# Head 0's first loads on the hardware queues, head 1's on GpSimd's, the block list ahead of both, and two mask transfers later

## The chip, the cores and the metric

The kernel runs on one core of one Trainium2 chip. The core has a matrix engine (TensorE, "PE" in the profile), a vector engine (VectorE, "DVE"), a scalar engine with activation functions (ScalarE, "ACT"), GpSimd ("POOL") and SyncE ("SP"). SP, ACT and GpSimd can each issue transfers (DMAs) to 16 DMA engines that they share. SP's and ACT's transfers go through hardware queues and copy data as it is; GpSimd's go through a software queue and may convert the type on the way, here from fp32 in memory to bf16 on the chip. The metric is the device time of one execution in microseconds (us), lower is better; the median of three runs before the change is 204.28 us.

## The reference

Block-sparse attention (BigBird's pattern) followed by a gated feed-forward layer with a short convolution. Sizes: batch 4, 8 heads, 768 tokens, head dimension 64, blocks of 32 tokens (24 blocks), three sampled blocks for each block; model width 512, inner width 1024.

```python
scores = (1/sqrt(D)) * q @ k.T                    # per batch and head
mask = |blk_i - blk_j| <= 1  or  blk_i, blk_j in {0, 23}
mask |= kb in sampled_blocks[qb]                  # the block list
attn = softmax(where(mask, scores, -1e9)) ;  a = attn @ v
x = a as (B, S, 512)
h = relu(x @ w_in)
conv = sum_k conv_w[k] * shift(h, k - 1)          # along the tokens
out = (h * sigmoid(conv)) @ w_out
```

## The kernel before, in words

**Units.** The 32 heads are handled as 16 pairs (4 batches of 4 pairs). For a pair, the scores are computed transposed, a 128x128 tile of (keys, queries) at a time; eight such tiles fill a tile `st` of 128x1024 and are one *unit*. A unit is: matmuls into `st` (line L746 of the profile), one exponential on ACT from `st` to `pt` (L757), and eight matmuls of `pt` with the values into `av` (L779). There are 144 units; a pair takes four and a half of them for the first half of the queries and as many for the second, and a unit is called by its number below (unit 0 is the first). Two `st` tiles alternate, so the scores of unit u can be written once the exponential of unit u-2 is done.

**The mask.** The mask is not applied after the scores but multiplied in. The tiles `e` and `o` hold, for one pair, keys and queries transposed (64 rows of features) and below them 24 more rows, one for each block: on the key side these rows say which blocks may not be looked at, on the query side they hold -8000 at the token's own block. The key side is made from the block list `sbi` on DVE (`a_rand`, L284 and L286, then `k_rows`, L314), the query side from `nblk` (`q_rows`, L300). Tiles `e` and `o` exist five times (slots 0 to 4, `e_67` to `e_71` and `o_72` to `o_76`). Slot 0's mask rows are computed, slot 1's copied on DVE (L358), and slots 2 to 4 are filled by six transfers that SP issues (L361, `m_dma`), 72 KB each. Pair 4, the first in slot 4, is needed from unit 36 on.

**The first loads.** Pair 0's queries and keys come as fp32 through the hardware queues into tiles `o2s`: SP issues head 0's keys (`k0`), then the block list, then the convolution's weights; ACT issues both heads' first 384 queries (`q0`) and then head 1's keys (`k1`). Four casts on ACT (`cast`, L328 as every copy of `dcopy`) turn them into the bf16 tile `nat_88`. All the other loads, pair 1's keys first, are GpSimd's (all recorded at L241), one after the other in an order fixed by `in_turn`.

**Transposes.** Keys and queries of pairs 0 to 4 are transposed on PE (keys L470, queries L508) into PSUM (`mix` or `av`) and copied from there into `e` and `o` by ACT or DVE (L328 or L330). Later pairs are transposed by transfers of SP (L585).

**The rest.** When the values of a pair are summed, DVE normalizes them (L696, L698), the result is transposed (L707 by SP, L717 by PE) and goes through the first feed-forward matmul (L895), the relu (L915 on ACT or L917 on DVE), the convolution and gate (L949 to L1006) and the second matmul (L825), whose result goes out. These steps run among the units of later pairs.

**What sets the order.** Every step is an `op` in a graph, and the table `ORDER` lists the steps by number, with the engine and the buffer where there is a choice. `put_down` writes the program in that order, so each engine's instructions stand in a fixed row and wait for each other by semaphores. On PE the first row is 44 `warm` matmuls of a zero tile (L1027), and 12 `fill` matmuls (L1034) stand among the first units.

## Time and profile before

| what | before |
|---|---|
| median of 3 runs | 204.28 us (203.92 to 204.41) |
| the profiled execution's own time | 204.64 us |
| its span, first to last instruction | 202.9 us |
| PE busy | 196.4 us, 97% |
| ACT busy | 188.0 us, 93% |
| DVE busy | 179.9 us, 89% |
| mean busy share of the DMA engines, 5 to 45 us | over 0.9 in most slices |

The span leaves out 1.74 us of the execution (204.64 less 202.9), which lie before the first and after the last instruction. Starts in the profile count from the span's start. In a row of the timeline stand start, length, engine, line, operation, written tile<-read tile, shape and count; in brackets the engine's idle time just before, and what ended it. Rows that hold several instructions run from the first one's start to the last one's end. "Busy" of PE contains the modelled time that a matmul takes through the array, so short gaps of PE do not show in it.

### The profile page before, as it was taken

The numbers are of one execution on the slowest core, as the hardware profiler recorded it, in microseconds if no ns is written. First come the engines' busy times: TensorE is split into PE (matmuls) and PEld (weight loads), VectorE is DVE, ScalarE is ACT, GpSimd is POOL, SyncE is SP. The second block draws the span as 40 slices with busy tenths as digits, with TensorE's granted clock in tenths as the row PEclk, the third lists the DMA queues.
The fourth block names the chain that finished last, engine by engine and source line by source line (L and its number), as shares of the span: only waits on it lengthen the run. The fifth ranks groups of instructions, "written<-read, shape, count | busy, mean of one in ns | idle before, by whom it ended". The sixth has DMA issues, their size and how long they took to land.

```text
span 202.9 us, 6808 instructions
## 1 busy us (share of the span) xinstructions
PE 196.4 (97%) x2707; PEld 153.6 (76%) x2707; DVE 179.9 (89%) x574; ACT 188.0 (93%) x247; POOL 56.3 (28%) x108
## 2 busy tenths in 40 slices
PE   7898999999999999999999999999999999999993
PEld 7797888897788777877688877776678877776742
DVE  8965989999999978999899988999899968999950
ACT  5898999999999999999999998999999989998842
POOL 8940789300621363102534328400000000000000
PEclk9999999999999999999999999999999999999999
DMA  6999999995879399947969699995331202001515
GB/s 147 167 217 200 179 178 186 192 145 118 120 117 143 75 120 157 212 108 154 128 103 165 71 214 211 123 155 137 93 116 23 42 14 68 13 11 58 200 62 206
DMA packets 53711, 26.11 MB, mean 129 GB/s; under 512 B 39624, under 2 KB 50592, under 8 KB 53680
## 3 DMA queue, kind: packets, MB, share of 16 engines
q0 software_dynamic: 19984, 11.24, 43.3%
q1 hardware_dynamic: 33136, 13.92, 34.9%
q10 hardware_dynamic: 560, 0.52, 0.7%
q8 instruction: 21, 0.34, 0.7%
q14 instruction: 10, 0.08, 0.1%
HBM read 23.08 MB, written 6.29 MB: 145 GB/s over the span
## 4 chain that ended last, share of the span: by engine, by line
PE 74%; ACT 14%; DMA 5%; POOL 3%; issue 3%; DVE 0%; ACTq 0%
PE st L746 23%; PE mix L895 18%; PE mix L825 17%; PE av L779 13%; ACT pt L757 12%; DMA nat<-in_q_dram 5%; POOL nat L241 2%; POOL vn L241 1%; PE mix L810 1%; PE st L825 1%; ACT m L998 1%; PE av L970 1%; ACT hE L915 1%; PE mix L508 1%; ACT o2s L328 0%
## 5 line engine op out<-in xcount | busy, mean ns | idle before, releaser
L757 ACT ACTIVATE pt<-st 128x1024 bf16<-128x1024 f32 x144 | 140.4, 1037 | 2.4 <-PE st L746 1.2
L779 PE MATMUL av<-vt,pt 128*128 128x65 bf16 x1152 | 59.7, 193 | 0.0
L779 PEld LDWEIGHTS <-pt 128*128 128x128 bf16 x1152 | 52.1, 97 | 9.9 <-ACT pt L757 0.3
L895 PE MATMUL mix<-xT,winb 128*128 128x384 bf16 (+2 forms) x288 | 53.7, 308 | 0.1
L949 DVE TENSOR_SCALAR m<-hE,cw 128x382 bf16<-128x382 bf16 (+2 forms) x192 | 49.4, 317 | 0.5 <-ACT hE L915 0.2
L825 PE MATMUL mix<-woutb,gT 128*128 128x512 bf16 x176 | 47.1, 379 | 0.0
L746 PE MATMUL st<-o 88*128 88x128 bf16 (+1 forms) x240 | 44.2, 229 | 0.4 <-ACT pt L757 0.3
L746 PE MATMUL st<-o,e 88*128 88x128 bf16 (+1 forms) x228 | 43.3, 233 | 0.2 <-ACT pt L757 0.2
L746 PE MATMUL st<-e,o 88*128 88x128 bf16 (+1 forms) x224 | 42.5, 234 | 0.5 <-ACT pt L757 0.5
L746 PE MATMUL st<-e 88*128 88x128 bf16 (+1 forms) x208 | 40.9, 239 | 0.3 <-ACT o L328 0.3
L746 PEld LDWEIGHTS <-o 88*128 88x128 bf16 x464 | 34.7, 97 | 8.4 <-issue 1.6
L746 PEld LDWEIGHTS <-e 88*128 88x128 bf16 x436 | 32.6, 97 | 7.0 <-ACT e L328 0.4
L959 DVE TENSOR_TENSOR m<-m 128x764 bf16<-128x764 bf16 (+2 forms) x64 | 33.6, 532 | 0.4
L895 PEld LDWEIGHTS <-winb 128*128 128x128 bf16 x288 | 23.9, 97 | 7.8 <-issue 0.5
L998 ACT ACTIVATE m<-m 128x764 bf16<-128x764 bf16 (+2 forms) x32 | 26.3, 830 | 0.5 <-DVE m L959 0.3
L417 POOL COPY pace<-pt 1x1 bf16<-1x1 bf16 x24 | 6.4, 267 | 56.1 <-ACT pt L757 56.0
L825 PEld LDWEIGHTS <-gT 128*128 128x128 bf16 x184 | 15.2, 97 | 8.7
L1006 DVE TENSOR_TENSOR gT<-m,hE 128x764 bf16<-128x764 bf16 (+3 forms) x36 | 18.1, 511 | 0.5
L698 DVE TENSOR_TENSOR xtok<-av,rcp 128x384 bf16<-128x384 f32 (+2 forms) x36 | 18.2, 506 | 0.3
L917 DVE TENSOR_SCALAR hE<-mix 128x384 bf16<-128x384 f32 x29 | 15.9, 550 | 2.5 <-PE mix L895 2.1
L915 ACT ACTIVATE hE<-mix 128x384 bf16<-128x384 f32 (+2 forms) x35 | 17.2, 508 | 0.7 <-PE mix L895 0.5
L241 POOL DMA_DIRECT2D nat<-in_q_dram x23 | 16.9, 736 | 2.7 <-issue 2.3
(80 smaller groups left out, 155.7 us busy)
## 6 DMA issues: line engine op xcount, KB each, us to landing
out_dram<-o2s SPq DMA_DIRECT2D x23, 256.0 KB
vn<-in_v_dram POOLq DMA_DIRECT2D x16, 192.0 KB, 5.6
nat<-in_k_dram POOLq DMA_DIRECT2D x15, 192.0 KB, 5.4
nat<-in_q_dram POOLq DMA_DIRECT2D x7, 192.0 KB, 5.2
winb<-in_moe_w_in_dram POOLq DMA_DIRECT2D x2, 512.0 KB, 11.7
woutb<-in_moe_w_out_dram POOLq DMA_DIRECT2D x4, 256.0 KB, 6.2
nat<-in_q_dram POOLq DMA_DIRECT2D x8, 96.0 KB, 4.6
nq<-in_q_dram POOLq DMA_DIRECT2D x5, 96.0 KB, 5.4
```

The source lines that it names most:

```text
L241: return op(name, {eng: occ}, lambda e: on(e).dma_start(out=dst(), in_=src), prio, deps, dma=(kind, service), **kw)
L698: nm = op("norm", {"DVE": t_dps(128 * C)}, lambda e: nc.vector.tensor_tensor(out=xtok_t[xk.index][:, 0:C].rearrange("p c h d -> p h c d"), ...
L746: nc.tensor.matmul(out=st[:, 128 * x:128 * (x + n_)], lhsT=QK[kc % 2][s][0:88, 1, hh, kc // 2, :], rhs=QK[par][s][0:88, 0, hh, idx:idx + n ...
L757: nc.scalar.activation(out=pt_t[ptb.index], in_=st_t[stb.index], func=AF.Exp, bias=0.0, scale=0.125)
L779: nc.tensor.matmul(out=o[:, off:off + 65], lhsT=pt_t[ptb.index][:, 128 * x:128 * x + 128], rhs=V_t[vslot_b[P].index][:, hh, kc, 0:65], sta ...
L825: nc.tensor.matmul(out=acc(), lhsT=gT_t[gb.index][:, ffc, 128 * t:128 * t + 128], rhs=woutb[:, ffc, :], start=(ffc == 0), stop=(ffc == NFF ...
L895: nc.tensor.matmul(out=mix_t[hb.index][:, w1 * y:w1 * y + w1], lhsT=winb[:, fc, 128 * ffc:128 * ffc + 128], rhs=xT_t[xt_buf[n].index][:, f ...
L915: i = nc.scalar.activation(out=dst, in_=src, func=AF.Relu, bias=0.0, scale=0.5)
L949: i = nc.vector.tensor_scalar(out=m_t[cb.index][:, x, y, 0:w], in0=hE_t[heb.index][:, f0 + y, t0 + x:t0 + x + w], scalar1=cw[:, x, f0 + y: ...
L959: nc.vector.tensor_tensor(out=m[:, a_, :, 0:w], in0=m[:, a_, :, 0:w], in1=m[:, b_, :, 0:w], op=ALU.add)
L998: th = [op("tanh", {"ACT": t_act(2 * w) + 0.04}, lambda e, cb=cb, w=w: nc.scalar.activation(out=m_t[cb.index][:, 0, :, 0:w], in_=m_t[cb.in ...
L1006: i = nc.vector.tensor_tensor(out=gT_t[gtb.index][:, f0:f0 + 2, t0:t1], in0=m_t[cb.index][:, 0, :, 0:w], in1=hE_t[heb.index][:, f0:f0 + 2, ...
```

## The change

Five things change.

1. SP issues the block list first and, behind it, head 0's queries alone (128x192 fp32, 96 KB). ACT issues head 0's keys as its only load.
2. Head 1's first queries and keys become GpSimd's first two loads and arrive as bf16 in `nat_88`. Two of the four casts are gone.
3. Before slot 4's two mask transfers stands a new step `slot_mem`: GpSimd writes two elements into `e_71` and `o_76`, so these transfers wait until GpSimd has come that far.
4. The table `ORDER` is another one. It differs up to unit 39 or so, and is the same from there on (the last difference on PE is row 1443 of 5415). In it pair 0's query rows of `e` go from DVE to ACT, the copies for the last batch's mask (`mlast`) go from the start to behind pair 3's copies, and one relu goes from DVE to ACT (28 instead of 27 on ACT of 128x384, 28 instead of 29 on DVE).
5. The code is four lines shorter above the units, so line numbers in the changed program are lower by 4 to 10 (L746 becomes L742, L757 L753, L508 L504, L328 L320, L361 L355).

```diff
 ORDER = """
-00010w0y020A0407080506q/1r0r10zr2r3030VA30ar4r5r6r7r80xr9rarb0drc1d0rdrerfrgrh090b0fV0gV0j0nVrirjrk0mVrlrm1ern
+00010w0y020A04050607q/109r0r1r2r3r403r5r6r70ar8r9rarb0brcrd0cre0T3rf08rgrh0U0Brirjrk1d00drl0g0eArm0WArn0fV0VA
...
-    qf, kf = o2s_t[0], [o2s_t[1], o2s_t[2]]
-    def first_q(e, prio, after):
-        return dma("ld_q0", e, lambda: qf[:, 0:384].rearrange("p (h c) -> p h c", h=2),
-                   q[0, 0:2, 0:384].rearrange("h (p c) d -> p h (c d)", p=128), prio, service=0.7, earliest=1.0, after=after)
-
-    def first_k(x, e, prio, after):
-        return dma("ld_k0", e, lambda: kf[x][:, 0:384], k[0, x].rearrange("(p c) d -> p (c d)", p=128), prio,
-                   service=0.75, earliest=1.0, after=after)
-
-    k0 = first_k(0, "SP", -22, [])
-    q0 = first_q("ACT", -22, [])
-    k1 = first_k(1, "ACT", -21, [q0])
+    qf, kf = o2s_t[0], o2s_t[1]
+    k0 = dma("ld_k0", "ACT", lambda: kf[:, 0:384], k[0, 0].rearrange("(p c) d -> p (c d)", p=128), -22,
+             service=0.75, earliest=1.0)
     ld_sb = op("ld_sb", {"SP": 0.46}, lambda e: nc.sync.dma_start(out=sbi, in_=sampled_blocks.bitcast(I32)), -21,
-               after=[k0], lat=1.8)
-    ld_q0, ld_k0 = [q0, q0], [k0, k1]
-    ld_cw = dma("ld_cw", "SP", lambda: cw0, moe_conv_w.rearrange("k (f p) -> (k f) p", p=128), 8, service=0.05, after=[ld_sb])
+               lat=1.8)
+    q0 = dma("ld_q0", "SP", lambda: qf[:, 0:192], q[0, 0, 0:384].rearrange("(p c) d -> p (c d)", p=128), -22,
+             service=0.5, earliest=1.0, after=[ld_sb])
+    ld_cw = dma("ld_cw", "SP", lambda: cw0, moe_conv_w.rearrange("k (f p) -> (k f) p", p=128), 8, service=0.05, after=[q0])
...
     for s in range(1, NSLOT):
-        mr = []
+        mr, late = [], []
+        if s == 4:
+            late = [op("slot_mem", {"POOL": 0.2}, lambda e, s=s: [nc.gpsimd.tensor_copy(out=t[s][64:65, 0, 0, 0, 0:2], in_=warm[64:65, 0:2]) for t in (E_t, O_t)], T(14), [o_warm])]
...
-                             T(4.5 * s - 2.5) + 0.1 * x, [m_h1[x], m_kh[x]] + m_k[1:] * x, dma=("hw", 0.6)))
+                             T(4.5 * s - 2.5) + 0.1 * x, [m_h1[x], m_kh[x]] + m_k[1:] * x + late, dma=("hw", 0.6)))
...
         if P == 0:
-            both = {"ACT": 0.42, "DVE": 0.47}
-            cq = [cast("cast_q", lambda x=x: nat_t[nb.index][:, 0, 192 * x:192 * x + 192],
-                       lambda x=x: qf[:, 192 * x:192 * x + 192], -16.5 + 2 * x, [ld_q0[x]], {"ACT": 0.25, "DVE": 0.28},
-                       uses=[nb]) for x in range(2)]
-            ck = [cast("cast_k", lambda x=x: nat_t[nb.index][:, 1, 384 * x:384 * x + 384], lambda x=x: kf[x][:, 0:384],
-                       -16.6 + 2 * x, [ld_k0[x]], both, alloc=[] if x else [nb],
-                       uses=[nb] if x else [])
-                  for x in range(2)]
-            ld_k, ld_q = ck, cq
+            lq = dma("ld_q1", "POOL", lambda: nat_t[nb.index][:, 0, 192:384],
+                     q[0, 1, 0:384].rearrange("(p c) d -> p (c d)", p=128), -22, service=0.3, kind="sw", alloc=[nb])
+            lk = dma("ld_k1", "POOL", lambda: nat_t[nb.index][:, 1, 384:768],
+                     k[0, 1].rearrange("(p c) d -> p (c d)", p=128), -21, service=0.55, kind="sw", uses=[nb])
+            in_turn("first", lq)
+            in_turn("first", lk)
+            cq = cast("cast_q", lambda: nat_t[nb.index][:, 0, 0:192], lambda: qf[:, 0:192], -16.5, [q0],
+                      {"ACT": 0.25, "DVE": 0.28}, uses=[nb])
+            ck = cast("cast_k", lambda: nat_t[nb.index][:, 1, 0:384], lambda: kf[:, 0:384], -16.6, [k0],
+                      {"ACT": 0.42, "DVE": 0.47}, uses=[nb])
+            ld_k, ld_q = [ck, lk], [cq, lq]
```

The order moves instructions at three places that the prediction speaks of. The first is the start of GpSimd's row, from the identity matrix to the queries of pair 3 (`nat_88` is pair 0's natural layout, `nat_85`, `nat_86` and `nat_87` are pairs 1, 2 and 3, `vn` holds values). Before:

```order
L263 AFFINE_SELECT ident<-ident 128x128
L241 DMA nat_85<-in_k_dram 128x2x384
L261 IOTA colidx_i 24x24
L241 DMA nat_85<-in_q_dram 128x2x192
L241 DMA vn_92<-in_v_dram 128x2x384
...
L241 DMA nat_87<-in_q_dram 128x2x192
```

And now:

```order
L255 AFFINE_SELECT ident<-ident 128x128
L241 DMA nat_88<-in_q_dram 128x192
L253 IOTA colidx_i 24x24
L241 DMA nat_88<-in_k_dram 128x384
L241 DMA nat_85<-in_k_dram 128x2x384
L241 DMA nat_85<-in_q_dram 128x2x192
L241 DMA vn_92<-in_v_dram 128x2x384
...
L241 DMA nat_87<-in_q_dram 128x2x192
```

Two loads stand ahead of pair 1's keys, and every later load is issued two places further back; pair 3's queries were the ninth load and are the eleventh.

The second is the start of ACT's row, up to the exponentials of the first units (`pt_96` is unit 0's, `pt_97` unit 1's; `mix` and `av` hold transposed keys and queries of pair 0). Before:

```order
L241 DMA o2s_125<-in_q_dram 128x2x192
L241 DMA o2s_127<-in_k_dram 128x384
L328 ACT_TABLE_LOAD
L328 CAST nat_88<-o2s_126 128x384
L328 CAST nat_88<-o2s_125 128x192 x2
L328 CAST nat_88<-o2s_127 128x384
L328 COPY e_67<-mix_65 64x384
L328 COPY e_67<-mix_66 64x256
L328 COPY o_72<-mix_66 64x128
L328 COPY o_72<-mix_65 64x384
L328 COPY e_67<-av_63 64x256
L757 ACTIVATE pt_96<-st_61 128x1024
```

And now:

```order
L241 DMA o2s_126<-in_k_dram 128x384
L290 ACT_TABLE_LOAD
L290 ACTIVATE e_67<-nblk 24x256
L290 ACTIVATE e_67<-nblk 24x128
L320 CAST nat_88<-o2s_126 128x384
L320 CAST nat_88<-o2s_125 128x192
L320 COPY e_67<-mix_65 64x384
...
L320 COPY o_72<-mix_65 64x384
L753 ACTIVATE pt_96<-st_61 128x1024
L320 COPY e_67<-av_64 64x384
L753 ACTIVATE pt_97<-st_62 128x1024
```

One load and two casts are gone, two small mask activations have come, and the copy that stood ahead of unit 0's exponential is now behind it, with head 1's keys in place of its queries.

The third is PE's row around the transposes of pair 3's queries (`nat_87`). Weight loads, which stand ahead of every matmul, are left out, and so are further matmuls of the same kind. Before:

```order
L746 MATMUL st_61<-o_74,e_69 128x128
...
L746 MATMUL st_61<-e_69,o_74 128x128
L508 MATMUL mix_66<-ident,nat_87 128x128
...
L779 MATMUL av_63<-vt_78,pt_103 128x65
...
L779 MATMUL av_63<-vt_78,pt_96 128x65
L746 MATMUL st_62<-e_69,o_74 128x128
```

And now:

```order
L742 MATMUL st_62<-e_69,o_74 128x128
...
L742 MATMUL st_62<-o_74,e_69 128x128
L775 MATMUL av_64<-vt_79,pt_97 128x65
...
L504 MATMUL mix_66<-ident,nat_87 128x128
...
L742 MATMUL st_61<-e_69 128x256
```

The transposes stood between the scores of unit 10 (`st_61`) and those of unit 11 (`st_62`); they now stand between unit 11's and unit 12's (`st_61` again), and no matmuls into `av` stand between them and unit 12's scores any more, where eight stood before unit 11's.

80 lines of the change are left out of this document (40 added, 40 removed).

## The prediction

> **What bounds the kernel now.** I read the page first, then the chain of waits in order of time, then the timeline of the first 20 us, and last the transfers by their time to landing.
>
> ```profile
> span 202.9 us, 6808 instructions
> PE 196.4 (97%) x2707; PEld 153.6 (76%) x2707; DVE 179.9 (89%) x574; ACT 188.0 (93%) x247; POOL 56.3 (28%) x108
> ```
>
> The two engines that bound it together are PE and ACT. By stages (columns: busy time of PE, its weight loads, DVE, ACT and POOL, then the granted clock, the share of the DMA engines and GB/s), they have little left from 18 us on, and nothing from 26 us:
>
> ```profile
> 18.00:26.00 8.00, 7.69 (x150) 7.13 (x147) 6.41 (x23) 7.36 (x9) 4.20 (x7) 1.00 1.19 185
> 26.00:40.00 14.00, 14.00 (x199) 11.44 (x196) 13.29 (x43) 13.81 (x18) 10.20 (x23) 1.00 1.33 187
> 40.00:60.00 20.00, 20.00 (x299) 16.01 (x298) 19.44 (x55) 19.95 (x25) 3.33 (x8) 1.00 0.95 132
> ```
>
> So a microsecond won or lost before 20 us reaches the end, since the work after unit 39 is the same in the same order. The chain of waits begins with loads (start, length, what):
>
> ```profile
> 1.41 0.83 POOL nat L241
> ...
> 7.33 10.12 DMA nat<-in_q_dram
> 18.13 0.46 PE st L746 x6
> ```
>
> GpSimd issues its loads one after the other, and pair 3's queries, issued at 7.33, land at 17.45. The timeline shows what that costs, and what comes first (start, length, then the idle time before in brackets):
>
> ```profile
> 0.74 0.40 SPq L241 DMA_DIRECT2D o2s<-in_k_dram  x1
> 3.78 1.61 ACT L328 CAST nat<-o2s 128x384 bf16<-128x384 f32 x4 [0.73 <-DMA o2s<-in_k_dram]
> 4.34 0.48 PE L470 MATMUL mix<-ident,nat 128*128 128x128 bf16 x3
> 5.29 0.73 ACT L328 COPY e<-mix 64x384 bf16<-64x384 bf16 x2
> 6.05 0.64 ACT L328 COPY o<-mix 64x128 bf16<-64x128 bf16 x2
> 6.32 0.27 PE L746 MATMUL st<-e 88*128 88x256 bf16 x1 [0.26 <-ACT o L328]
> 7.36 0.37 ACT L328 COPY e<-av 64x256 bf16<-64x256 bf16 x1 [0.67 <-DVE o L330]
> 7.63 10.39 ACT L757 ACTIVATE pt<-st 128x1024 bf16<-128x1024 f32 x11
> 17.49 0.40 PE L508 MATMUL mix<-ident,nat 128*128 128x128 bf16 x4 [0.64 <-DMA nat<-in_q_dram]
> 18.67 1.02 ACT L757 ACTIVATE pt<-st 128x1024 bf16<-128x1024 f32 x1 [0.64 <-PE st L746]
> ```
>
> Two places decide. At the start ACT waits 0.73 us for head 0's keys, works through four casts and four copies, waits 0.67 us for DVE, and starts unit 0 at 7.63. Eleven exponentials then run without a gap, about 0.92 us apart. At 17.49 PE gets pair 3's queries late and ACT loses 0.64 us before unit 11 at 18.67; unit 12 follows 0.92 us later, at 19.59.
>
> **The start, part by part.** The sum is made on the profiled execution, 204.64 us, of which 202.9 are span; the median of the runs is 0.36 us lower, and I take the change off the median.
>
> Head 0's keys move from SP's queue to ACT's, where they are still the first thing issued. They landed just before 3.78, three microseconds after their issue, and I let them land at the same time; with half the bytes beside them it could be 0.3 us earlier, behind the other queue 0.4 us later. Two of four casts go: half of 1.61 is 0.80, so ACT would be free at 4.58, but PE's key transposes end at 4.34 + 0.48 = 4.82, and the copies start at 4.85 instead of 5.29. They take the same 1.40 us (5.29 to 6.69), so ACT is done at 6.25. Unit 0's scores start when the third copy is done, 5.88 instead of 6.32; from there to the last of unit 0's matmuls 0.6 us pass, so unit 0's exponential starts at about 6.5, 1.1 us earlier. The copy of 0.37 us that stood ahead of it with its wait on DVE now stands behind it, on 384 columns instead of 256, and holds up unit 1: 6.5 + 0.92 + 0.38 = 7.8, against 7.63 + 0.92 = 8.55. **From unit 1 on the start is worth 0.75 us** (0.35 to 1.05 by the landing of the keys).
>
> The mask rows that ACT takes over (`q_rows`, 24x256 and 24x128) run while ACT waits for the keys; ahead of them ACT loads a table:
>
> ```profile
> 1.76 1.28 ACT L328 ACT_TABLE_LOAD   x1 [1.76 <-issue]
> ```
>
> The table load ended at 3.04 and now comes some 0.5 us earlier because one issue ahead of it is gone, so 1.2 us are idle for two operations that took DVE 0.47. If that cover were gone, they would cost their length. DVE hides the rest, and only just:
>
> ```profile
> 2.23 0.47 DVE L300 TENSOR_SCALAR e<-nblk 24x256 bf16<-24x256 bf16 x2
> ...
> 3.17 0.66 DVE L344 TENSOR_SCALAR mlast<-nblk 24x128 bf16<-24x128 bf16 x3
> ...
> 4.74 0.21 DVE L284 TENSOR_TENSOR hit<-colidx_i,sbi 24x72 f32<-24x72 int32 x1
> ...
> 10.53 0.77 DVE L330 COPY o<-mix 64x256 bf16<-64x256 bf16 x2
> ```
>
> DVE works with hardly a gap up to 11.3, where pair 1's last copy ends; unit 4, whose second half needs the copy before it, started at 7.63 + 4 x 0.92 = 11.3. In the change unit 4 is wanted 0.75 us earlier, and DVE has 0.47 + 0.66 = 1.13 us less to do before, so it keeps up with 0.4 us to spare. This needs the block list before the compare (L284). It is issued at 0.74 now; even if it landed only when the keys did, just before 3.78, the compare would run 0.9 us earlier than at 4.74, which is still enough. Zero in the sum.
>
> **Head 1 on GpSimd.** Two loads, of 48 and 96 KB as bf16, go ahead of pair 1's keys. What GpSimd's loads cost (KB, and microseconds from issue to landing), first in an empty queue late in the kernel, then the loads issued at 1.41 (pair 1's keys), 6.62 (pair 3's keys) and 7.33:
>
> ```profile
> nq<-in_q_dram POOLq DMA_DIRECT2D x1, 96.0 KB, 2.9
> nat<-in_k_dram POOLq DMA_DIRECT2D x1, 192.0 KB, 3.8
> ...
> nat<-in_k_dram POOLq DMA_DIRECT2D x1, 192.0 KB, 4.7
> nat<-in_k_dram POOLq DMA_DIRECT2D x1, 192.0 KB, 7.3
> nat<-in_q_dram POOLq DMA_DIRECT2D x1, 96.0 KB, 10.1
> ```
>
> Head 1's keys, issued second at about 2.34, land between 5.2 (empty queue) and 7.0 (as pair 1's keys did). PE wants them behind unit 0's scores, at 6.5; unit 1 is due at 7.8 and needs 0.4 us of transposes and 0.45 of scores ahead, so they are hidden up to 6.9, and I add nothing.
>
> **Pair 3's queries.** They move from the ninth load to the eleventh. From pair 1's keys (landed 6.1) to pair 3's (13.9) 1152 KB came in, 148 KB for each microsecond; so 144 KB more are at most 0.97 us. It is less where GpSimd starts on a freer queue: pair 1's keys are then issued two issues (1.6 us) later, at 3.0, and land at 6.8 if they take the 3.8 of an empty queue, 0.7 us later, or 0.3 us later if the queue fills faster. Against that stand the two mask transfers of slot 4, 144 KB, which no longer come into this stretch; they cancel the whole 0.97 if they were moved ahead of or beside pair 3's queries, and give nothing if they queued behind. Ends: 0.65 us earlier (0.3 less 0.97) and 0.97 later. The stretch around their landing is the busiest one:
>
> ```profile
> 8.00:12.00 4.00, 3.46 (x60) 3.24 (x58) 3.71 (x10) 4.00 (x5) 3.53 (x6) 1.00 1.24 172
> 12.00:16.00 4.00, 4.00 (x83) 3.72 (x81) 2.12 (x8) 3.89 (x5) 0.92 (x2) 1.00 1.36 231
> ```
>
> GB/s go from 172 to 231 there though GpSimd issued only two more loads, so something else, and the masks are all that is open, moves beside pair 3's queries and not after them. I take the end near cancellation: 0.2 us later, 17.65.
>
> The Trainium skill has a rule on this ("DMA: Bandwidth & Descriptors", section "Queues, rings and completion order"): each DMA engine takes packets in turn from all the queues that have work for it. By it the masks take turns with pair 3's queries whenever they were issued, the landing would not move from 17.45, and the sum would come to 203.3; with strict order of issue it would be 18.4 and 204.3. The stretch of 231 GB/s agrees with turns.
>
> What hangs on it: unit 11 started 18.67 - 17.45 = 1.22 us after the landing, with the eight `av` matmuls (0.25 us) between. Now unit 12 comes in this place without them: 17.65 + 0.97 = 18.6. Without any wait unit 12 would start at 19.59 - 0.64 - 0.75 = 18.2. So 0.4 us of the wait stay, and **at unit 12 the kernel is 19.59 - 18.6 = 1.0 us ahead.**
>
> **One relu more on ACT.** Between unit 12 and unit 39 ACT does one relu that DVE did:
>
> ```profile
> 40.69 0.51 ACT L915 ACTIVATE hE<-mix 128x384 bf16<-128x384 f32 x1
> 41.06 1.96 ACT L757 ACTIVATE pt<-st 128x1024 bf16<-128x1024 f32 x2
> ```
>
> It takes 0.37 us of ACT (40.69 to 41.06). It costs nothing where PE holds ACT up, and all of it where ACT is the bound; in the stage from 26 to 40 us ACT has 0.19 us idle, and I take 0.2 of 0.37. The `slot_mem` step, two copies of two elements on GpSimd, and the wait of the later mask transfers cost nothing: behind them on SP stands only a transpose that ran at 38.11, and slot 4 is needed from unit 36 on. The first and the last mask transfer and that transpose were issued here:
>
> ```profile
> 7.10 0.89 SPq L361 DMA_DIRECT2D e<-e  x1
> ...
> 11.07 0.71 SPq L361 DMA_DIRECT2D o<-o  x1
> ...
> 38.11 1.30 SPq L707 DMA_TRANSPOSE xT<-xtok  x1
> ```
>
> **Sum:** 1.0 less 0.2 is 0.8 us: 203.8 in the profiled execution, **203.5 us** as the median.
>
> **Rivals.**
>
> *The wait eats it all* (20%). Pair 3's queries land at 18.4, with nothing won from the masks. Unit 12 starts at 19.4 and 0.2 us are left, which the relu takes: 204.3. For it: nothing but queue order is needed. Against it: the stretch of 231 GB/s.
>
> *The masks go ahead of pair 3's queries, slower* (13%). The masks of slots 2 and 3 wait for DVE (the first one was issued at 7.10, the others 0.8 us apart), which is now a microsecond earlier, while pair 3's queries are issued 1.4 us later. In order of issue only one mask stood ahead of them; now four do, 216 KB more, 1.46 us at 148 KB. The landing goes to 17.45 + 0.97 + 1.46 = 19.9, unit 12 to 20.85, 1.26 us behind, and with the relu the time is 205.7. It decides from a landing of 18.4 on, where unit 12 comes no earlier than before, and from 19.0 on the kernel is measurably slower.
>
> *No wait remains* (8%). The load lands by 17.2 and unit 12 starts at 18.2, 1.4 us ahead: 202.9, or 202.6 if the keys come 0.3 us earlier.
>
> *A colder matrix engine* (4%). The first row of `warm` matmuls is 25 long and no longer 30, so PE idles 0.6 us before its first transposes, at 4.34, and no longer 0.16:
>
> ```profile
> 1.06 3.12 PEld L1027 LDWEIGHTS <-warm 128*128 128x128 bf16 x30 [1.06 <-DVE warm L225]
> 6.71 0.49 PEld L1027 LDWEIGHTS <-warm 128*128 128x128 bf16 x7
> ```
>
> A `warm` takes 0.104 us at first and 0.07 or less from about 5 us on, though the row of the granted clock shows nothing of it. If the faster pace came later, units 0 and 1 would take twice their 0.46 us, about 0.9 us in all, and the time would be 204.4. The Trainium skill ("TensorE: Matmul & The Clock Gate", section "What's actually happening") says that the clock opens after a window of some 3.4 us in which PE was busy, and starts anywhere in it; whether an idle 0.6 us matters it does not say, and no row here shows it.
>
> **How the numbers follow.** My forecast has 55%, its own range is 202.8 to 203.9. A measurement here can tell about 0.3%, 0.61 us: faster is below 203.67, slower above 204.89. Faster: 52 of the forecast's 55 and the 8 without a wait, 0.60. Same: 3, 20 and 4, 0.27. Slower: 0.13. The range of 202.6 to 204.8 leaves out most of the slower rival and little below.
>
> **What would show it.** In the changed profile: casts that start near 3.8 and two fewer; unit 0 at about 6.5 and unit 1 at 7.8; the compare before 3.8; pair 3's transposes after a wait, at 17.7, and unit 12 at 18.6; from there to the end the same distance as before plus 0.2 us. I am wrong if unit 1 starts after 8.2 (keys late), if unit 4 waits for DVE (list late), or if pair 3's queries land after 18.4.

## The result, and the profile after

The change makes the kernel slower, by 0.67%. The median is 205.69 us (205.01 to 206.26, five executions) against 204.2 (203.92 to 204.41) for the kernel before beside it; the ratio is 1.0067, 95% interval 1.0042 to 1.0092. The forecast was 203.5 in a range of 202.6 to 204.8. Timed once more (e17), the change had a median of 205.32 us, ratio 1.006 (1.0029 to 1.0091). Some executions of either kernel took over 1.5% longer than the fastest of their kernel; medians, ranges and ratios leave them out.

The profiled execution is the slowest of the five, 206.26 us. The page has PE and ACT no busier than the longer span explains, and DVE less busy than before:

```profile
span 204.5 us, 6815 instructions
PE 197.8 (97%) x2707; PEld 154.5 (76%) x2707; DVE 178.5 (87%) x571; ACT 188.7 (92%) x248; POOL 56.9 (28%) x112
```

The timeline of the changed kernel up to 16 us (start, length, then the idle time before in brackets):

```profile
3.24 0.77 ACT L320 CAST nat<-o2s 128x384 bf16<-128x384 f32 x2 [0.15 <-DMA o2s<-in_k_dram]
4.10 0.95 PE L1023 MATMUL st<-warm 128*128 128x128 bf16 x7
5.44 0.37 ACT L320 COPY e<-mix 64x256 bf16<-64x256 bf16 x1 [0.63 <-PE mix L504]
5.70 0.89 SPq L355 DMA_DIRECT2D e<-e  x1
5.95 0.42 PE L742 MATMUL st<-e 88*128 88x256 bf16 x1
7.05 1.02 ACT L753 ACTIVATE pt<-st 128x1024 bf16<-128x1024 f32 x1 [0.58 <-PE st L742]
8.33 5.70 ACT L753 ACTIVATE pt<-st 128x1024 bf16<-128x1024 f32 x6
13.98 0.40 PE L504 MATMUL mix<-ident,nat 128*128 128x128 bf16 x4 [0.89 <-DMA nat<-in_q_dram]
15.03 2.01 ACT L753 ACTIVATE pt<-st 128x1024 bf16<-128x1024 f32 x2 [1.00 <-PE st L742]
```

The keys came early (ACT waited 0.15 us, not 0.73), but seven `warm` matmuls stand between the transposes of the keys and those of the queries, and PE was slow: unit 0's first score matmul took 0.42 us here and 0.27 before. Unit 1 started at 8.33, not at 7.8. Then six exponentials ran without a gap, and at unit 7 ACT lost 1.00 us, because **pair 2's** queries were not there. The chain of waits shows them as its longest piece by far:

```profile
5.59 0.85 POOL nat L241
6.44 7.49 DMA nat<-in_q_dram
13.93 0.05 issue
13.98 0.40 PE mix L504 x4
...
19.94 0.83 ACT pt L753
```

Issued at 6.44, they landed at 13.93. Before, they were issued at 5.19 and landed 5.7 us later, at 10.9 (transfers by size and time to landing):

```profile
nat<-in_q_dram POOLq DMA_DIRECT2D x1, 96.0 KB, 5.7
```

Pair 3's queries, on which the forecast hung, landed at 16.3, and nothing waited for them. The first mask transfer was issued at 5.70, ahead of pair 2's queries; before, at 7.10, it stood behind pair 3's keys.

Unit 12's exponential starts at 19.94, 0.35 us behind the profile before; 1.1 us more are lost between units 44 and 64, where the chain of the same profile has one transfer by the crossbar (one that transposes on its way, issued by SP for a later pair):

```profile
52.81 1.25 SPq L581
54.06 0.05 issue
54.15 5.80 DMA stg<-nat
```

### The profile page after: what moved, and what is told of

It reads as the page before. It is cut to its first block, busy times and chain, and to the rows that moved or that the text cites. A ratio compares the mean times of both kernels' runs of the same rounds, so it can differ in the third digit from the quotient of the medians.

```text
span 204.5 us, 6815 instructions
## 1 busy us (share of the span) xinstructions
PE 197.8 (97%) x2707; PEld 154.5 (76%) x2707; DVE 178.5 (87%) x571; ACT 188.7 (92%) x248; POOL 56.9 (28%) x112
## 4 chain that ended last, share of the span: by engine, by line
PE 70%; DVE 11%; DMA 6%; ACT 6%; POOL 3%; issue 2%; SPq 1%; DVEq 0%; ACTq 0%
PE st L742 22%; PE mix L821 17%; PE mix L891 16%; PE av L775 12%; ACT pt L753 5%; DMA nat<-in_q_dram 4%; DMA stg<-nat 3%; DVE m L945 3%; DVE m L955 2%; POOL nat L241 2%; DVE e L322 2%; DVE o L322 1%; PE mix L806 1%; PE st L821 1%; DVE xtok L694 1%
## 5 line engine op out<-in xcount | busy, mean ns | idle before, releaser
L753 ACT ACTIVATE pt<-st 128x1024 bf16<-128x1024 f32 x144 | 140.4, 1035 | 4.0 <-PE st L742 3.2
L775 PE MATMUL av<-vt,pt 128*128 128x65 bf16 x1152 | 60.5, 193 | 0.1
L742 PE MATMUL st<-o 88*128 88x128 bf16 (+1 forms) x240 | 44.0, 229 | 0.3 <-ACT pt L753 0.3
L742 PE MATMUL st<-o,e 88*128 88x128 bf16 (+1 forms) x228 | 43.6, 234 | 0.4 <-DVE o L322 0.2
L742 PE MATMUL st<-e,o 88*128 88x128 bf16 (+1 forms) x224 | 42.5, 234 | 0.0
L742 PE MATMUL st<-e 88*128 88x128 bf16 (+1 forms) x208 | 41.3, 241 | 0.1
L742 PEld LDWEIGHTS <-o 88*128 88x128 bf16 x464 | 34.7, 97 | 7.2 <-issue 0.6
L742 PEld LDWEIGHTS <-e 88*128 88x128 bf16 x436 | 33.1, 98 | 8.7 <-issue 1.9
L911 ACT ACTIVATE hE<-mix 128x384 bf16<-128x384 f32 (+2 forms) x36 | 17.8, 510 | 0.7 <-PE mix L891 0.5
L241 POOL DMA_DIRECT2D nat<-in_q_dram x24 | 17.5, 731 | 1.8 <-issue 1.5
L913 DVE TENSOR_SCALAR hE<-mix 128x384 bf16<-128x384 f32 x28 | 15.3, 550 | 2.9 <-PE mix L891 2.6
```

The costliest lines, as they stand in the source:

```text
L241: return op(name, {eng: occ}, lambda e: on(e).dma_start(out=dst(), in_=src), prio, deps, dma=(kind, service), **kw)
L742: nc.tensor.matmul(out=st[:, 128 * x:128 * (x + n_)], lhsT=QK[kc % 2][s][0:88, 1, hh, kc // 2, :], rhs=QK[par][s][0:88, 0, hh, idx:idx + n ...
L753: nc.scalar.activation(out=pt_t[ptb.index], in_=st_t[stb.index], func=AF.Exp, bias=0.0, scale=0.125)
L775: nc.tensor.matmul(out=o[:, off:off + 65], lhsT=pt_t[ptb.index][:, 128 * x:128 * x + 128], rhs=V_t[vslot_b[P].index][:, hh, kc, 0:65], sta ...
L911: i = nc.scalar.activation(out=dst, in_=src, func=AF.Relu, bias=0.0, scale=0.5)
```

## The experiments

The table gives, by profile, the start of the exponentials of units 1 and 12, and what was left of the span from the latter on. The times beside it are medians; (one) is a single execution.

| run | unit 1 | unit 12 | rest | time, us | ratio (95%) |
|---|---|---|---|---|---|
| before, profile of the forecast | 8.55 | 19.59 | 183.3 | 204.2 | 1 |
| e5, before again | 8.54 | 18.80 | 184.5 | 205.12 (one) | |
| after | 8.33 | 19.94 | 184.5 | 205.69 | 1.0067 (1.0042 to 1.0092) |
| e6, after again | 8.03 | 21.00 | 186.9 | 209.72 (one) | |
| e17, after again | 8.17 | 20.54 | 183.4 | 205.32 | 1.006 (1.0029 to 1.0091) |
| e1, masks of slots 2, 3 later | 7.51 | 19.15 | 183.4 | 205.02 | 1.004 (1.0015 to 1.0066) |
| e3, all masks as before | 7.42 | 20.19 | 183.6 | 205.76 | 1.0062 (1.0035 to 1.0089) |
| e4, before, slot 4's masks late | 8.52 | 18.77 | 183.6 | 204.12 | 0.9998 (0.9985 to 1.0011) |
| e7, before, two loads first | 8.04 | 21.35 | 183.6 | 207.72 | 1.0207 (1.0139 to 1.0275) |
| e8, head 1 on hardware queues | 8.30 | 18.77 | 183.2 | 204.38 | 1.0008 (0.9983 to 1.0033) |
| e10, before, GpSimd 1.2 us later | 8.13 | 22.52 | 183.2 | 206.41 | 1.0112 (1.0079 to 1.0145) |
| e14, e10 with masks later | 8.14 | 20.23 | 183.3 | 205.28 | 1.0052 (1.0034 to 1.007) |
| e15, before, 25 warm | 9.60 | 19.86 | 183.4 | 204.56 | 1.0017 (0.9996 to 1.0037) |
| e13, after, 30 warm | 7.69 | 19.49 | | 204.57 | 1.0025 (1.0004 to 1.0046) |

The rest is 183.2 to 183.6 us in ten of these thirteen; what the edits do is, in the main, in the start of unit 12. The other three (e5, after, e6) have a late crossbar transfer in it, and so has e13, whose rest is left out for it.

**The two kernels once more.** No edit (e5, e6, and e17 at the end).

> The kernel before, unchanged, profiled a second time. The forecast rested on one profile of it, in which pair 3's queries landed at 17.44 us and ScalarE lost 0.64 us ahead of unit 11; 15 of the 16 parts of that load had landed by 15.1. Theory A (that landing is where this load ends in most executions): it lands at 17.0 to 17.9 again and unit 11 starts near 18.67. Theory B (one part that came late in that one execution): it lands by 16.3, unit 11 starts near 17.9, and the span is 0.4 to 0.8 us shorter than 202.9, 202.1 to 202.5 us.

> The changed kernel, unchanged, profiled a second time; the profile at hand is that of the slowest of its five executions, 206.26 us against a median of 205.69. Theory A (both losses belong to the kernel): unit 7 waits 0.8 us or more for pair 2's queries again, and the distance to the kernel before grows by 1 us between units 39 and 59 again. Theory B (what belongs to the kernel is that units 4 to 11 run up against the loads, and which load is waited for changes from execution to execution; the loss between units 39 and 59 was an accident): unit 0 starts anywhere from 6.1 to 7.05 us, as TensorE's pace changes early or late, units 4 to 11 lose 0.8 us or more against their own start at one or another load or mask, and the distance does not grow by more than 0.3 us behind unit 39.

The chain of waits of e5, the kernel before, from two stretches of time:

```profile
core 0 of [0], span 203.3 us
...
18.80 0.84 ACT pt L757
...
53.07 5.79 DMA stg<-nat
```

Its pair 3's queries, issued at 7.31, and their time to landing:

```profile
nat<-in_q_dram POOLq DMA_DIRECT2D x1, 96.0 KB, 7.3
```

For e5 theory B holds in the landing and in unit 11 (17.89). No load stands in its chain ahead of unit 12: pair 3's queries landed at 14.6, and unit 12 came 0.79 us earlier than in the profile of the forecast. The span, 203.3 us, is longer than B had it, since e5 has the same late crossbar transfer as the changed kernel (5.79 and 5.80 us) and the same loss of 1.1 us behind it. So that loss comes without the change too, and the wait of 0.64 us ahead of unit 11 does not come in every execution of the kernel before. e6 bears out neither theory as a whole: unit 7 waits as in A, and behind unit 39 the distance to the profile before grew by 3.4 us, against B, with a crossbar transfer of 8.65 us in the chain. In e17 that distance stays within 0.02 us from unit 39 to unit 64, so that loss is not in every execution of the change either. Six profiles of the changed start have unit 1 at 7.42 to 8.33 (after, e1, e2, e3, e6, e17). In e6 unit 4 waited 0.73 us for v and unit 7 1.47 for pair 2's queries; e17 waited for the latter again, which were 8.08 us under way:

```profile
core 0 of [0], span 203.9 us
...
6.45 8.08 DMA nat<-in_q_dram
...
20.54 0.83 ACT pt L753
```

**Masks of slots 2 and 3 later (e1), slot 4's earlier (e2), both (e3), and slot 4's late in the kernel before (e4).** In e1 and e3 GpSimd writes two elements of slot 2's tile behind the issue of pair 2's queries, for which the first mask transfer waits; in e2 and e3 slot 4's wait is gone:

```diff
+        also(gr.ops[92], E_t[2])     # pair 2's queries: a copy of two elements behind the issue
...
-                             ... + m_k[1:] * x + late, dma=("hw", 0.6)))
+                             ... + m_k[1:] * x, dma=("hw", 0.6)))
```

> The changed kernel, but the four mask transfers of slots 2 and 3 wait until GpSimd has issued pair 2's queries (about 7.2 us), so that they are issued 1.5 us later than in the changed kernel, at about the time at which they were issued before. Theory A (the masks move beside pair 2's loads and make them late): pair 2's queries land by 12.9 us instead of 13.93, the wait of 1.0 us ahead of unit 7 is gone or below 0.3, and unit 9 starts by 16.4 instead of 17.21; masks now move beside pair 3's queries, which may cost up to 0.6 of it again: 204.7 to 205.3 us. Theory B (two more loads ahead and the issue 1.25 us later are enough to make them late): they still land at 13.6 or later, unit 9 stays at 17.1, 205.7 us.

> The changed kernel, but slot 4's two mask transfers are issued right behind those of slot 3 (about 8.9 and 9.7 us), and the two copies on GpSimd that held them back do nothing. Theory A (the loss behind unit 44 comes from slot 4's masks, which now move at 22 to 24 us beside GpSimd's loads): GpSimd's loads of 25 to 47 us land 1 to 1.9 us earlier, the distance to the kernel before no longer grows between units 39 and 59, and the time is about 1.1 us less, 204.6 us, if pair 2's and pair 3's loads don't get later by more than 0.3. Theory B (the loss behind unit 44 comes from the later start alone, a collision of the crossbar transposes with whatever moves then): it stays, 205.5 to 205.9 us.

> Both of the edits above: all six mask transfers are issued at the times at which the kernel before issued them, and only the start (the keys on ScalarE's queue, head 1 by GpSimd) and the order stay changed. If the masks make both losses: pair 2's queries land by 12.9, the loss behind unit 44 is gone, 203.6 to 204.2 us. If the two loads of head 1 make the first loss: 204.4 to 204.8 us. If neither loss comes from the masks: 205.7 us.

> The kernel before, with the one edit that slot 4's two mask transfers wait for GpSimd to have issued the second quarter of the output weights (about 22.3 us). Theory A (late masks of slot 4 cost by themselves): GpSimd's loads behind 25 us land 1 us or more later, the crossbar transposes between 38 and 60 us take longer, and the time rises by 0.6 to 1.1 us, 204.8 to 205.3 us. Theory B (they cost nothing by themselves): pair 3's queries land up to 0.9 us earlier than 17.44 because 144 KB less move ahead of them, and the time is 203.6 to 204.3 us.

In e1 (timeline first, then the transfers by time to landing) pair 2's queries took 5.3 us and landed at 11.8, and the wait ahead of unit 7 is gone. It came back two units later:

```profile
7.63 0.90 SPq L355 DMA_DIRECT2D e<-e  x1
15.83 0.22 PE L742 MATMUL st<-o,e 88*128 88x128 bf16 x1 [0.83 <-DMA o<-o]
16.42 6.52 ACT L753 ACTIVATE pt<-st 128x1024 bf16<-128x1024 f32 x7 [1.16 <-PE st L742]
```

```profile
nat<-in_q_dram POOLq DMA_DIRECT2D x1, 96.0 KB, 5.3
```

Now the masks of slot 2 themselves are late for unit 9. For e1 theory A holds in the landing and in the time (205.02 us, though its ratio can't be told from the change's): with the masks first issued at 5.7 us pair 2's queries landed at 13.4 to 15.0 (six profiles), with 7.63 at 11.8 and 12.7 (e1, e3). It failed in e3, which with every mask as before lost as much as the change (205.76), by pair 0's v at unit 4, the masks at unit 9 and pair 3's keys at unit 10. In the changed kernel moving the masks back changed who was late, with no difference in the time that can be told from none. Slot 4's late masks cost nothing: e4 equals the kernel before, and e2, which has them early, was not measurably faster than the change (205.03 us, between the times of its two theories; ratio 1.0053, 1.0024 to 1.0081).

**Two loads at the head of GpSimd's queue (e7), the same delay without bytes (e10), and that with the masks' place kept (e14).** All on the kernel before:

```diff
+        # e7: behind op 10 (ident)
+        nc.gpsimd.dma_start(out=gT_t[1][:, 0, 0:192], in_=q[0, 1, 0:384]...)
+        nc.gpsimd.dma_start(out=gT_t[1][:, 1, 0:384], in_=k[0, 1]...)
+        # e10, e14 instead: four nc.gpsimd.affine_select(out=gT_t[1][:, x, 0:128], in_=warm, ...)
+        # e14: a copy of two elements into E_t[2] behind the issue of pair 3's keys
```

> The kernel before with GpSimd issuing two loads more ahead of pair 1's keys: head 1's queries and keys, 48 and 96 KB as bf16, once more, into a tile that is not used until much later; nothing waits for them. It measures by itself what two loads at the head of GpSimd's queue cost. Theory A (the load stream bounds units 4 to 11, and each load behind the two comes about 1 us later): pair 2's queries land at 11.9 or later (10.94 before), pair 3's at 16.5 or later, units 9 to 12 start 0.5 to 1.2 us later than in the kernel before, 204.7 to 205.4 us. Theory B (the two loads have room): 204.2 us within 0.3.

> The kernel before, with four more operations of 0.3 us on GpSimd ahead of its first load (they fill a tile that is not used until much later), so that its loads are issued about 1.2 us later, as with two loads ahead, but no byte more is loaded. Theory A (the later issue costs, the bytes little): pair 1's first values land 1.5 us or more later than at 7.96, units 4 to 11 wait for loads, and the time is above 205.5 us, near the 207 of the run with two loads ahead (e7). Theory B (the 144 KB cost, the issue little): the loads land 0.5 us or less later from pair 2 on, because the stream catches up, and the time is 204.0 to 204.6 us.

> The kernel of e10 (the kernel before, GpSimd's loads 1.2 us later), and the mask transfers wait until GpSimd has issued pair 3's keys, so that they stand behind that load as they did in the kernel before (there 0.5 us behind it). Theory A (the loads were late because masks had come ahead of them): pair 3's keys land by 15.5 us instead of 17.18, the wait of 1.86 us for them is gone; if then the masks of slot 2 are in time as well, 204.4 to 205.4 us, and if unit 9 waits for them instead, 205.5 to 206. Theory B (a later load stream costs by itself): pair 3's keys land at 16.5 or later and the time stays at 206 to 207 us.

The two loads cost more than even theory A allowed: 2.1% of the time by the ratio, 1.3% by the lower two of its four executions (206.67 and 206.86; the others took 208.58 and 209.71). By the timeline of e7 ScalarE waits at units 4, 5, 6 and 9, for pair 0's v at unit 4, then pair 2's keys and queries, and pair 3's keys at unit 9:

```profile
10.60 0.52 PE L779 MATMUL av<-vt,pt 128*128 128x65 bf16 x12 [0.74 <-DVE vt L330]
12.02 1.02 ACT L757 ACTIVATE pt<-st 128x1024 bf16<-128x1024 f32 x1 [1.14 <-PE st L746]
13.42 0.40 PE L508 MATMUL mix<-ident,nat 128*128 128x128 bf16 x4 [0.18 <-DMA nat<-in_q_dram]
17.57 0.51 PE L470 MATMUL mix<-ident,nat 128*128 128x128 bf16 x6 [0.89 <-DMA nat<-in_k_dram]
```

The delay alone (e10) costs 1.1%, which is half of the 2.1 and most of the 1.3. Its profiled execution is the longest of four (205.49 to 207.54 us). Its chain, and below it the stages (the columns are those of the forecast's table of stages; the granted clock is the third figure from the right):

```profile
7.80 9.38 DMA nat<-in_k_dram
17.18 0.05 issue
17.22 0.68 PE mix L470 x6
17.90 0.85 PE st L746 x6
```

```profile
16.00:18.00 2.00, 0.78 (x8) 0.72 (x9) 0.07 (x1) 0.37 (x1) 0.00 (x0) 0.86 1.39 199
18.00:20.00 2.00, 2.00 (x24) 1.81 (x23) 1.38 (x5) 1.02 (x1) 0.00 (x0) 0.50 1.26 205
```

Pair 3's keys, issued 1.2 us later, landed at 17.18, against 13.9 before. PE had idled for 1.86 us by then, its granted clock fell to 0.50, and unit 12 came at 22.52. The first mask had been issued at 6.68, ahead of the keys. In e14 it stands behind them (9.02), and theory A is borne out in the landing: the keys take 7.5 us, land at 15.3, and that wait is gone.

```profile
nat<-in_k_dram POOLq DMA_DIRECT2D x1, 192.0 KB, 7.5
```

The masks, last in turn now, hold unit 9 (for that case theory A gave 205.5 to 206 us; 205.28 was measured):

```profile
9.96 6.91 DMA o<-o
...
20.23 0.83 ACT pt L757
```

Unit 12 is still 1.43 us later than in e5, for 1.2 us of later issue.

**Head 1 on the hardware queues (e8).** The changed kernel, with its start, its masks' code and its order; only head 1 comes otherwise:

```diff
-            lq = dma("ld_q1", "POOL", ...
-            lk = dma("ld_k1", "POOL", ...
+            lq = cast("cast_q", lambda: nat_t[nb.index][:, 0, 192:384], lambda: o2s_t[3][:, 0:192], ..., {"DVE": 0.28}, ...)
+            lk = cast("cast_k", lambda: nat_t[nb.index][:, 1, 384:768], lambda: o2s_t[2][:, 0:384], ..., {"DVE": 0.47}, ...)
+        also(k0, nc.scalar, o2s_t[2][:, 0:384], k[0, 1]...)       # second on ScalarE's queue
+        also(q0, nc.sync, o2s_t[3][:, 0:192], q[0, 1, 0:384]...)  # third on SyncE's queue
```

> The changed kernel, but head 1's first queries and keys come by the hardware queues (keys second on ScalarE's, queries third on SyncE's) and are cast by VectorE between its mask copies, so that GpSimd's first load is pair 1's keys again, issued at 1.4 us. The new start, the mask times and the order stay. Theory A (the two loads at the head of GpSimd's queue are what turns the gain into a loss): pair 2's queries land by 11.7, pair 3's by 16.6, unit 12 starts by 18.6 and the time is 203.0 to 203.8 us. Theory B (the masks, which are still issued from 5.7 us on, or the new order make the loss): 204.6 us or more.

The chain of e8 has no load of GpSimd any more:

```profile
1.65 4.29 DMA o2s<-in_q_dram
...
18.77 0.83 ACT pt L749
```

204.38 us, ratio 1.0008: the loss is gone, as theory A had it, though the median is above its 203.0 to 203.8. The profiled execution (203.73) is one of four at 203.64 to 203.74; the other six took 204.38 to 205.34. This run moves two things: GpSimd's loads are issued 1.0 to 1.3 us earlier again, and the masks later (6.79), since DVE has two casts ahead of them. Which of them does more e8 doesn't tell; by e10 and e14 the later issue and the masks' place are about half each of what the delay costs.

**The pace of PE: the queries' transposes ahead of seven warm matmuls (e9 on e8, e11 on the change), 30 warm matmuls instead of 25 ahead of the keys (e12 on e8, e13 on the change), and 25 instead of 30 in the kernel before (e15).** The edits move rows of PE; e12 and e13, by the order of PE:

```
 MATMUL st<-warm   x25                MATMUL st<-warm   x30
 MATMUL mix<-ident,nat  x3 (keys)     MATMUL mix<-ident,nat  x3 (keys)
 MATMUL st<-warm   x7                 MATMUL st<-warm   x2
 MATMUL mix<-ident,nat  x2 (queries)  MATMUL mix<-ident,nat  x2 (queries)
```

> The kernel of the run with head 1 on the hardware queues (e8), and the two transposes of head 0's queries stand directly behind the three of its keys, ahead of the seven warm matmuls that stood between them (0.95 us in the changed kernel). Theory A (with GpSimd's first load at 1.4 us again the loads leave room, so that an earlier start reaches the end): ScalarE's copy of the queries starts 0.6 us earlier, unit 1 starts at 7.3 to 7.8 us instead of 8.30, unit 12 at 18.0 to 18.3 instead of 18.77, and the time is 203.0 to 203.6 us, below the kernel before. Theory B (units 4 to 11 can't start earlier than in the kernel before, whatever the start gains, because the loads land when they do): unit 1 is earlier, unit 12 is at 18.6 or later, 203.9 to 204.4 us.

> The changed kernel with the same move alone: the transposes of head 0's queries directly behind those of its keys. Theory A (units 4 to 11 are held up by the loads): unit 1 starts 0.4 to 0.8 us earlier than in the changed kernel at the same pace of TensorE, at 7.3 to 7.9 us, and the waits at units 4 to 9 grow by as much: unit 12 stays at 19.9 or later and the time at 205.2 to 206 us. Theory B (the start is worth what it gains): unit 12 by 19.4 and 204.6 to 205.0 us.

> The kernel with head 1 on the hardware queues (e8), and five of the seven warm matmuls between the transposes of head 0's keys and queries stand ahead of the keys' transposes, so that the first row is 30 long as in the kernel before and TensorE's idle 0.55 us there is filled. Theory A (the shorter first row exposes the pace, and the seven matmuls delay the queries' transposes): the pace changes before 6 us, ScalarE copies the queries 0.4 us earlier than in e8, unit 1 starts at 7.3 to 7.9 us, the spread shrinks to that of the kernel before and the median is 203.2 to 203.7 us, below the kernel before. Theory B (the spread comes from the loads): 203.6 to 205.3 us as in e8, median 204.2 to 204.6.

> The changed kernel with the same five warm matmuls moved ahead of the keys' transposes. Theory A (its loss is the loads): unit 1 starts 0.3 to 0.8 us earlier than at 8.33, units 4 to 9 wait for loads and masks by so much more, 205.2 to 206 us. Theory B (the cold pace is a large part of the loss): 204.3 to 204.9 us.

> The kernel before, with five of the 30 warm matmuls ahead of the keys' transposes moved behind the queries' transposes, so that TensorE idles 0.6 us more before its first transposes, as in the change. Theory A (a gap there delays the change of pace, and what is delayed shows): the pace changes at 6 us or later, unit 0 starts up to 0.5 us later than at 7.63, the median rises by 0.2 to 0.8 us and the spread grows beyond 1 us. Theory B (the moment of the change has nothing to do with the gap, and the kernel before hides it behind ScalarE's casts): 204.1 us within 0.25 and a spread of 0.6 us.

In e15 PE idles ahead of the keys' transposes (row 2; more than in the kernel before), and seven warm matmuls beyond 7 us still take 0.95 us; unit 1 starts 1.05 us later than in the kernel before:

```profile
1.07 2.85 PE L1027 MATMUL st<-warm 128*128 128x128 bf16 x25 [1.07 <-DVE warm L225]
4.33 0.50 PE L470 MATMUL mix<-ident,nat 128*128 128x128 bf16 x3 [0.42 <-ACT nat L328]
7.82 0.95 PE L1027 MATMUL st<-warm 128*128 128x128 bf16 x7
8.06 1.02 ACT L757 ACTIVATE pt<-st 128x1024 bf16<-128x1024 f32 x1 [0.35 <-PE st L746]
9.60 2.86 ACT L757 ACTIVATE pt<-st 128x1024 bf16<-128x1024 f32 x3 [0.51 <-PE st L746]
```

The same seven in the timeline of the kernel before:

```profile
6.82 0.56 PE L1027 MATMUL st<-warm 128*128 128x128 bf16 x7
```

By the start times of single matmuls in the traces (0.107 us apart at first, 0.056 later) the pace changed 2.7 to 4.8 us after PE's first matmul in the nine profiles with 30 warm matmuls, and 3.0 to 9.5 us after it in the ten with 25. The late ones show: 8.3 us in e15, and 9.5 in e9, whose earlier transposes were lost to it (unit 1 at 9.43 and not at 7.3 to 7.8; 204.43 us, ratio 1.0019, 0.9997 to 1.004). Theory A of e15 holds for the profile and fits the time (204.56, spread 1.4 us); that the median rises is not settled, as the ratio's interval of 0.9996 to 1.0037 holds 1. In e13 the time is 204.57 us, as its theory B had it, and the ratio 1.0025, less than the change's 1.0067 and 1.006, with intervals that overlap a little: the late pace is probably part of the change's loss, 0.7 to 0.9 us by the ratios. The 0.25% that is left is clear of none (1.0004 to 1.0046), and in e13's profile units 4 and 7 still wait for v and pair 2's queries (0.80 and 0.39 us). e11 doesn't decide: unit 12 at 19.62, between its theories, and 205.49 us, ratio 1.0076 (1.0051 to 1.0102). e12 has its pace early and unit 0 at 6.44 in its profile, and still unit 12 only at 19.44. Its median is 203.71 us, ratio 0.9989 (0.9969 to 1.001): five of nine executions took 203.66 to 203.71, less than any of the 33 of the kernel before beside it (203.81 at least), and four took 204.41 to 204.79, the profiled one (204.75) among them. So that profile doesn't show the better ones, and what parts the two groups stays open.

**Head 1's queries third on ScalarE's queue (e16 on e12), and the change timed beside it (e17).**

```diff
-        also(q0, nc.sync, o2s_t[3][:, 0:192], q[0, 1, 0:384]...)
+        also(k0, nc.scalar, o2s_t[3][:, 0:192], q[0, 1, 0:384]...)
```

> The kernel of e12, but head 1's queries are issued third on ScalarE's queue, behind head 1's keys, instead of third on SyncE's. Theory A (their late landing was what held VectorE and the mask copies): VectorE no longer waits for them, unit 1 starts at 7.3 to 7.7 us, the masks are issued by 6.6 us, and the median is 203.0 to 203.7 us. Theory B (units 4 to 11 can't be earlier than in the kernel before because of the loads): unit 12 stays at 18.6 or later and the time at 203.6 to 204.4 us.

> The changed kernel, unchanged, timed beside e16. If its loss is what the first five executions showed: 205.3 to 206 us, ratio 1.005 to 1.009, and in the profile a wait for v, pair 2's queries or the masks of slot 2 between units 4 and 9 again. If those five were unlucky: 204.4 to 205 us, as e13.

```profile
1.65 0.45 ACTq L1033 DMA_DIRECT2D o2s<-in_q_dram  x1
6.47 0.53 DVE L322 CAST nat<-o2s 128x192 bf16<-128x192 f32 x2 [1.01 <-DMA o2s<-in_q_dram]
11.85 1.02 ACT L749 ACTIVATE pt<-st 128x1024 bf16<-128x1024 f32 x1 [0.55 <-PE st L738]
```

Theory A fell: whichever queue issues it, this transfer, issued at 1.65, lands at 5.9 (e8) to 6.4 us (e16), and DVE waits 0.33 us (e8) to 1.01 us (e16) for it. 204.45 us, ratio 1.002 (0.9993 to 1.0047). e17 confirms the change's loss. No version was shown to be faster than the kernel before; the nearest is e12.

## Why the prediction was wrong

**The profile of before.** The first failed step is the one that the gain hung on: "At 17.49 PE gets pair 3's queries late and ACT loses 0.64 us". That was one execution. In e5, the same kernel, the load is in time and unit 12 starts at 18.80; so it is in e4 (18.77), where slot 4's masks come later. The forecast took 0.8 us off an execution that had this wait, and put the result at the median; that most executions do not have the wait is likely (204.64 us for the one with it, 204.2 in the median, 204.12 for e4's profiled one) and not shown. Against 18.8, even its own unit 12 at 18.6 is a gain of 0.2 us, no change that can be measured.

**The start.** "Unit 0 at about 6.5 and unit 1 at 7.8" is the middle of what six profiles showed (6.14 to 7.05 and 7.42 to 8.33). The sum let the copies of the queries follow those of the keys at once; seven `warm` matmuls stand between, and ACT waited 0.63 us there in the profile of the result. The spread was missing too: it follows the pace of PE, from 4.1 us on the clock of the trace (e3, unit 1 at 7.42) to 7.0 (after, 8.33). The rival of the colder matrix engine named this with 4% and priced it at 0.9 us; e15 shows 1.05 in the kernel before. The Trainium skill ("TensorE: Matmul & The Clock Gate", section "What's actually happening") lets the clock open after a window of some 3.4 us of activity that starts anywhere; 2.7 to 4.8 us after the first matmul agrees with it roughly, 8.3 and 9.5 do not, unless the idle time ahead of the keys' transposes cost a further window, which no run here shows.

**"Pair 3's queries"** were priced alone, and this second failed step is where the loss comes from: two loads more ahead, at most 0.97 us later. They landed at 16.3, earlier than forecast. But each load behind the two is later, and the first that is wanted sooner than it can come sets the time: pair 2's queries, 13.9 to 15.0 in the three profiles of the change against 10.9 and 10.4. The forecast looked at one landing, the last, because it was the one with a wait in its row. It put the later issue of the loads between at nothing; without a byte more, e10 and e14 measure 1.1% of the time for it with the masks ahead of pair 3's keys, and 0.5% with the masks behind. The reading of the 231 GB/s was wrong as well: between 12 and 16 us the masks were not "all that is open", for five of GpSimd's loads, issued from 6.62 to 9.73, landed at 13.9 to 19.0. So that stretch does not show where the masks move: the 0.2 us has no ground in it, and the sum of 203.3 no support. In e10 and e14 the masks' place moved the landing of pair 3's keys by 1.8 us (17.18 and 15.34).

**"Head 1's loads are hidden"** was right for the two loads themselves (head 1's keys landed at 5.1 and were wanted behind unit 0's scores), and wrong for what stands behind them.

**The slower rival,** "The masks go ahead of pair 3's queries", had its price nearly right, 205.7, and its mechanism: masks issued 1.4 us earlier, loads 1.2 us later, so that masks stand ahead of loads that they stood behind; e10 against e14 shows that mechanism on the kernel before (9.4 against 7.5 us to landing). Its place was wrong, pair 2's queries in place of pair 3's, and it was given 13%. That its time and the median agree to 0.01 us is luck: with the masks put back (e3) the loss stayed. (The rival without a wait leaves the relu's 0.2 us out of its 202.9.)

**The rest** held. DVE kept up at the start (the compare of the block list ran at 2.53), the mask rows on ACT cost nothing (ACT still waited 0.15 us for the keys behind them), and the relu's 0.2 us is at most 0.1: between units 12 and 40 the distance grows from 0.35 to 0.45 us against the profile of the forecast and not at all against e5. The late crossbar transfer came in single executions of both kernels; how often it comes in each is not known.

So the time of the change is this: unit 12 at 19.9 and 20.5 (21.0 in e6, an execution of 209.72 us) instead of 18.8. The two loads at the head of GpSimd's queue are the main cause (e7 makes a loss, and a larger one, in the kernel before; e8, which moves them and with them the masks, undoes it in the change): they make the later loads late themselves (e14) and put masks ahead of them (e10 against e14). The exposed pace of PE is a likely second (e13). How the median's loss divides between the two stays open.

## What to carry to other kernels

A load put at the head of a queue delays every load behind it, so price each of them against the time at which it is wanted, not only the one that the profile shows waiting. Where a stretch of transfers is full, moving one ahead can make another late: in the changed kernel, moving the masks back changed which unit waited, not the time. And a wait that rests on one landing in one profile needs a second profile before a gain is built on it.

## What the runs showed of the hardware

- After an idle of 1.86 us PE's granted clock was 0.50 for the next 2 us and more (from 18 to 20 us in e10). The Trainium skill ("TensorE: Matmul & The Clock Gate", section "Why this matters for your kernels") warns of gaps above some 3 us; here it fell after less, and such a wait can cost more than its length. The length alone does not decide: after idles of 2.28, 2.66 and 2.33 us that ended at 62.5 to 62.9 us (e2, e11, e13) the clock fell to 0.50, and after this one of 2.54 us in e6 it stayed at 1.00:

```profile
64.18 0.28 PE L742 MATMUL st<-e 88*128 88x256 bf16 x1 [2.54 <-DVE e L322]
```

- The late pace of the start is not in the row of the granted clock (1.00 from the first slice on), only in the length of the matmuls: 0.42 us against 0.27 for the same 88x256 one.
- The crossbar transfer `stg<-nat` that starts between 53 and 55 us takes 5.8 us in some executions (after, e5) and 8.65 to 8.86 in others (e2, e6, e11, e13), and what follows in the chain waits for it; in e8 and e17 it is not in the chain at all. What sets it off was not tried.
- A transfer of 96 KB issued at 1.65 us on a hardware queue landed at 5.9 to 6.4 us (e8, e16), while one of the same size issued 0.4 us earlier on SyncE's queue was cast from 3.66 on (after). Between the two issues came GpSimd's first load, at 1.41, and in e8 and e16 head 1's keys, issued at 1.17, are ahead as well; which of them is the reason was not tried.
